# Rebuilding the first batch's key chain in a fused attention and feed-forward kernel

## The chip, the cores and the metric

The kernel runs on one core of one Trainium2 chip. The metric is the device time of one execution in microseconds (us), as a median of several executions. Before the change the median is 321.27 us over three runs (320.65 to 321.33). The profiled execution of the kernel before took 322.2 us, with a profiled span of 320.4 us. All positions below are microseconds from the start of a profiled span.

## The reference, cut to what matters

```python
# q, k, v: (4, 4, 1088, 32) float32; S1, S2: (8, 32)
def phi(x):                                   # 64 features from 32 numbers
    a = einsum('rd,bhsd->bhsr', S1, x)
    b = einsum('rd,bhsd->bhsr', S2, x)
    return einsum('bhsi,bhsj->bhsij', a, b)   # 8 x 8
kv  = sum over s of phi(k) v;  z = sum over s of phi(k)
num = phi(q) kv;  den = phi(q) z + 1e-06
x   = num / den                               # bridged to (4352, 128)
out = ((x @ w1) * (x @ w2)) @ w3 @ w_out      # d_ff = 1024
```

The sketches S1 and S2 and the weights arrive as float64 words and are converted on the chip. The denominator is the delicate part. The kernel gets z from the Gram matrix of the keys, G, the sum over s of k kᵀ, through S1 G S2ᵀ. To keep enough bits, it splits each key k into a leading part k1, rounded on a grid of eight bits, and a rest k2 = k - k1.

## The kernel before

The 1088 positions of a head are handled as 1024 "main" ones (eight chunks j of 128) and 64 "rest" ones (those of two batches share a tile). TensorE's array is used in four column groups, one for each head h. The products of a half batch (four chunks) run in this order:

```python
def products(out, lhs, rhs, start):
    for i, c in enumerate(chunks):
        for h in range(H):                       # the four column groups in turn
            nc.tensor.matmul(out[h * D:(h + 1) * D], c[lhs][rows, h], c[rhs][rows, h], ...)
products(acc["kv"], "v", "kp", first)            # float32, 64 wide
products(acc["g2"], "k2", "ks", False)           # float32, 32 wide; ks = k + k1
products(acc["g1"], "k1", "k1", False)           # bf16, 32 wide
...
nc.scalar.mul(ym, acc["g2"], 0.5)                # G = g1 + (g2 + its transpose) / 2
nc.vector.transpose(yt, ym)
```

A float32 matmul of this program leaves two records in the trace, a bf16 one leaves one. "Record" below means such a record.

Weights are converted in chunks of 128 x 512: ScalarE makes two words (cv_c, cv_m) and for most chunks a tile of signs (sgn). VectorE joins them (w, wo, w3c). The matmuls "idle_ps" multiply zeros. They exist to keep TensorE's clock up. The first two groups of queries of batch 0 are written out by hand in one fixed order (the "first part"); later groups are merged by weights.

```python
run_all([..., kv0, q_tr, kv1, kvr, lambda: idle(8), q_lead, cv[0], fin1, lambda: idle(4), sketch_P,
         cv[1], fin2, fin4, lambda: idle(4), n_nat, cv[2], cv[3], fin3, ...
         f[2], n_dens, f[3], n_phi, f[4], n_phT, f[5], n_nd])     # six of the eight pairs of group 0
run(merge([(1.7, x) for x in f[6:]] + ffn_steps(1, 16), k_steps(1), w_out))
```

## Time and profile before

| what | kernel before |
|---|---|
| median of three runs | 321.27 us |
| profiled span | 320.4 us |
| first xT (attention output of group 0) starts | 40.35 us |
| VectorE starts on the keys of batch 1 | 57.40 us |
| last transpose of a w_out chunk ends | 114.94 us |
| from there to the end | 205.46 us |
| TensorE, VectorE, ScalarE busy | 293.6, 195.3, 132.7 us |

The page divides the span into 40 slices and prints the busy share of each engine in tenths. The chain of waits is read from the end of the execution back to its start, each piece being what released the next. The table of windows gives busy microseconds of each engine in a stretch. Those lines are in the prediction below. One more table of windows matters later, which shows only the instructions that write the tile ps_kvz, that is the Gram and feature-value matmuls. These are the kernel before's lines for one half batch and for one rest (window, its length, TensorE busy with its records, weight loads, VectorE, ScalarE, clock, DMA):

```profile
145.68:146.65 0.97, 0.97 (x80) 0.84 (x64) 0.00 (x0) 0.00 (x0) 1.00 0.00 0
155.43:155.75 0.32, 0.31 (x20) 0.27 (x16) 0.00 (x0) 0.00 (x0) 1.00 0.00 0
```

Each window runs from the start of the stretch's first record to the start of the next other record. The reader should keep 0.97 us for 80 records and 0.32 us for 20: 12.1 and 16 ns a record.

### The profile page before, as it was taken

Reading aid. Unit: us, or ns where it says so; the run is one execution under the profiler, and the core shown is the slowest. Engines: PE = TensorE matmul, PEld = TensorE weight load, DVE = VectorE, ACT = ScalarE, POOL = GpSimd, SP = SyncE. Lnnn points to the kernel's source line nnn. Section 1 sums busy time; section 2 is a strip of 40 time slices with the busy share of each in tenths; the row PEclk is TensorE's granted clock in tenths of the full one; section 3 lists DMA queues with packets and bytes.
Section 4 is the critical chain, followed back from the end, with each engine's and each line's share of the span. In section 5 each row is a group of like instructions: output and inputs, shape, how many; then the busy total and the mean of one; then the engine's idle time right before and its main releaser. Section 6 shows DMA issues by size and latency. Waiting matters only on the chain.

```text
span 320.4 us, 4951 instructions
## 1 busy us (share of the span) xinstructions
PE 293.6 (92%) x1924; PEld 174.4 (54%) x1924; DVE 195.3 (61%) x495; ACT 132.7 (41%) x258; POOL 16.6 (5%) x21
## 2 busy tenths in 40 slices
PE   7866997669998999999999999999999999999992
PEld 5746553257766765465645446555454644444581
DVE  6987867996879638376846626654572572462130
ACT  4313273897998330533332253322324224323231
POOL 2200000100003000010301001000100100000000
PEclk9855699978999999999999999999999999999998
DMA  5998240375743000000000000000000000000000
GB/s 165 337 264 243 94 133 0 105 266 163 246 156 118 0 0 2 33 1 2 3 33 2 0 33 0 2 2 35 2 0 0 33 0 2 33 0 1 35 33 17
DMA packets 15064, 20.77 MB, mean 65 GB/s; under 512 B 4032, under 2 KB 11456, under 8 KB 15040
## 3 DMA queue, kind: packets, MB, share of 16 engines
q1 hardware_dynamic: 15040, 20.46, 19.9%
q8 instruction: 15, 0.25, 0.3%
q14 instruction: 9, 0.07, 0.1%
HBM read 18.22 MB, written 2.23 MB: 64 GB/s over the span
## 4 chain that ended last, share of the span: by engine, by line
PE 73%; ACT 11%; DVE 10%; issue 4%; POOL 1%; DVEq 0%; POOLq 0%
PE ps_o L740 19%; PE a_ps L727 15%; PE b_ps L731 14%; PE ps_w3o L375 3%; PE ps_x L682 3%; ACT cv_c L230 3%; PE ps_kvz L474 3%; PE ps_c L610 3%; PE ps_ph L665 2%; PE ps_c L608 2%; PE idle_ps L184 2%; ACT sgn L236 2%; PE ps_ab L424 2%; ACT cv_m L231 1%; ACT ffa L729 1%
## 5 line engine op out<-in xcount | busy, mean ns | idle before, releaser
L733 DVE TENSOR_TENSOR ab<-ffa,b_ps 128x512 f32<-128x512 f32 (+1 forms) x72 | 47.2, 655 | 62.5 <-PE b_ps L731 56.9
L729 ACT COPY ffa<-a_ps 128x512 f32<-128x512 f32 (+1 forms) x72 | 40.7, 565 | 78.3 <-PE a_ps L727 73.4
L727 PE MATMUL a_ps<-xT,w 128*128 128x512 f32 (+1 forms) x144 | 72.4, 585 | 0.7 <-ACT xT L685 0.7
L731 PE MATMUL b_ps<-xT,w 128*128 128x512 f32 (+1 forms) x144 | 70.5, 571 | 1.3 <-ACT ffa L729 1.3
L740 PE MATMUL ps_o<-ab,w3o 128*128 128x512 f32 (+1 forms) x144 | 70.3, 582 | 0.7 <-ACT ob L743 0.7
L731 PEld LDWEIGHTS b_ps<-xT,w 128*128 128x128 f32 x144 | 26.7, 190 | 29.4 <-issue 22.7
L740 PEld LDWEIGHTS ps_o<-ab,w3o 128*128 128x128 f32 x144 | 24.8, 190 | 22.6 <-issue 20.2
L727 PEld LDWEIGHTS a_ps<-xT,w 128*128 128x128 f32 x144 | 24.4, 192 | 18.0 <-issue 11.7
L375 PE MATMUL ps_w3o<-wo,w3T 128*128 128x128 f32 x128 | 18.0, 293 | 2.4 <-ACT w3T L370 1.7
L264 DVE TENSOR_REDUCE g_q<-qT 128x1 f32<-128x512 f32 (+1 forms) x9 | 5.9, 655 | 23.3 <-ACT qT L578 23.3
L375 PEld LDWEIGHTS ps_w3o<-wo,w3T 128*128 128x128 f32 x128 | 16.9, 205 | 5.5 <-ACT w3T L370 2.8
L667 ACT COPY pT<-ps_ph 128x512 f32<-128x512 f32 (+1 forms) x18 | 9.2, 565 | 15.8 <-PE ps_ph L665 15.8
L231 ACT ACTIVATE cv_m<-raw 128x512 int32<-128x512 uint32 x22 | 15.4, 698 | 0.8 <-DVE w3c L248 0.8
L230 ACT ACTIVATE cv_c<-raw 128x512 f32<-128x512 f32 x22 | 15.4, 706 | 0.0
L610 PE MATMUL ps_c<-Rl,qT 128*128 128x96 f32 (+1 forms) x72 | 15.0, 302 | 0.0
L608 PE MATMUL ps_c<-Rf,q 128*128 128x64 f32 (+1 forms) x72 | 13.2, 276 | 1.4 <-POOL q L584 1.4
L584 POOL TENSOR_TENSOR q<-qT,q 128x512 f32<-128x512 f32 (+1 forms) x6 | 6.4, 1073 | 150.1 <-DVE q L275 150.1
L608 PEld LDWEIGHTS ps_c<-Rf,q 128*128 128x128 f32 (+1 forms) x72 | 11.4, 201 | 4.3 <-issue 2.4
L236 ACT CAST sgn<-cv_c 128x512 f16<-128x512 f32 x17 | 13.4, 790 | 0.1
L184 PE MATMUL idle_ps<-zeros 128*128 128x256 bf16 x52 | 11.9, 420 | 1.6 <-DVE zeros L179 1.6
L665 PEld LDWEIGHTS ps_ph<-ident,ph 128*128 128x128 f32 x68 | 7.9, 143 | 7.6 <-issue 5.9
L432 DVE TENSOR_TENSOR kp<-ps_ab,b_sb 128x1024 f32<-128x1024 f32 x8 | 9.8, 1222 | 3.5 <-ACT b_sb L428 3.5
(169 smaller groups left out, 372.8 us busy)
## 6 DMA issues: line engine op xcount, KB each, us to landing
raw<-in_moe_w_dram SPq DMA_DIRECT2D x20, 512.0 KB, 4.5
k_sb<-in_k_dram SPq DMA_DIRECT2D x4, 512.0 KB, 5.1
v_sb<-in_v_dram SPq DMA_DIRECT2D x4, 512.0 KB, 5.8
q_sb<-in_q_dram SPq DMA_DIRECT2D x4, 512.0 KB, 6.3
out_dram<-oT SPq DMA_DIRECT2D x8, 256.0 KB, 2.0
raw<-in_moe_w_out_dram SPq DMA_DIRECT2D x2, 512.0 KB, 10.4
kr<-in_k_dram SPq DMA_DIRECT2D x4, 32.0 KB, 3.7
vr<-in_v_dram SPq DMA_DIRECT2D x4, 32.0 KB, 6.0
```

The lines of the kernel that those rows point to most:

```text
L184: nc.tensor.matmul(idle_ps[:, :n], zeros[:, :128], zeros[:, :n], start=True, stop=True)
L230: nc.scalar.mul(x["c"], hi.bitcast(F32), 2.0 ** -112)
L231: nc.scalar.mul(x["m"].bitcast(I32), lo.bitcast(U32), 2.0 ** -29)
L236: nc.scalar.copy(bview(x["s"].bitcast(F16)[:, 1:], [[2, CW]]), x["c"])
L375: nc.tensor.matmul(ps, w3T[ko][:, c], wo[:, c], start=(c == 0), stop=(c == NC - 1))
L608: nc.tensor.matmul(C[rows, :2, j], s["q2"][:, cols], cols_of(Rf, b), start=True, stop=False, skip_group_check=True)
L610: nc.tensor.matmul(C[rows, :, j], s["qT"][:, cols], cols_of(Rl, b), start=False, stop=True, skip_group_check=True)
L727: nc.tensor.matmul(a_ps[:, :n], w1[:, cols], xT[key], start=True, stop=True)
L729: nc.scalar.copy(a_sb[:, :n], a_ps[:, :n])
L731: nc.tensor.matmul(b_ps[:, :n], w2[:, cols], xT[key], start=True, stop=True)
L733: nc.vector.tensor_mul(ab[:, :n], a_sb[:, :n], b_ps[:, :n])
L740: nc.tensor.matmul(o_ps[g][:, :n], w3o[:, c], ab_sb.pop((g, c))[:, :n], start=c == 0, stop=c == NC - 1)
```

## The change

The intent is to get the first batch's state ready earlier and to take work off ScalarE. Cut to its core:

```diff
-            products(acc["g2"], "k2", "ks", False)          # f32 32 wide
-            products(acc["g1"], "k1", "k1", False)          # bf16 32 wide
+            for h in range(H):                              # for each chunk
+                products(acc["g"], h, kk[rows, 0, h], kk[rows, :, h], start=start)   # k1 x [k1|k2], f32 64 wide
+                if kf is not None:
+                    products(acc["g2"], h, kk[rows, 1, h], kf[rows, h])              # k2 x k, f32 32 wide
+                else:                                       # rest keys: k2 x k1, k2 x k2
+                    for x in range(2):
+                        products(acc["g2"], h, kk[rows, 1, h], kk[rows, x, h])
...
-            nc.scalar.mul(ym, acc["g2"], 0.5)
-            nc.vector.transpose(yt, ym)
-            nc.vector.tensor_add(ym, ym, yt)
-            nc.vector.tensor_add(gb, gb, ym)
+            nc.vector.tensor_add(gb, gb, acc["g2"])
...
-            round_to(s["q1"], s["qT"], grid(s["qT"], 128, 8, "q"))
+            nc.scalar.activation(s["q2"], s["qT"], ACT.Identity, bias=g)
+            nc.scalar.activation(s["q1"], s["q2"], ACT.Identity, bias=g, scale=-1.0)
...
-            words, join, add = convert(n, dst, n % 4 != 1)
+            words, join, add = convert(n, dst, signs=False)  # w_out chunks: no sign cast
...
-    load_raw(NRAW)                                           # then k, v, q of batch 1, rests
+    load_raw(2)                                              # the others behind a memset after G
...
+             ... f[4], n_phi, w_out[1][1], f[5], n_phT, f[6], n_nd, f[7]])   # all eight pairs
-    run(merge([(1.7, x) for x in f[6:]] + ffn_steps(1, 16), k_steps(1), w_out))
+    run(merge(ffn_steps(1, 16), k_steps(1), w_out[2:]))
```

The rest keys also share the grid of an even batch's main keys now, so their own peak and rounding go; ks goes too. The sketch's masked copies move from GpSimd to ScalarE, raw buffers go from five to six, idle matmuls from 52 to 95, and the transfer queue is pinned to the order in which the first part is written. The first part was pinned on the compute engines before too. Below, "the gate" is the memset that holds the bulk loads (weights, inputs of batch 1) back until G is done.

## The prediction

> **What bounds the kernel now.** I read the page first, for engines and slices of the span (320.4 us, so a slice is 8.0 us). Rows below: busy tenths of TensorE and VectorE, the granted TensorE clock, the DMA share.
>
> ```profile
> PE   7866997669998999999999999999999999999992
> ...
> DVE  6987867996879638376846626654572572462130
> ...
> PEclk9855699978999999999999999999999999999998
> DMA  5998240375743000000000000000000000000000
> ```
>
> TensorE is full from slice 13 on; before that it has holes, and twice half a clock. All that the change can win lies in the first 115 us. Next the chain of waits in the prologue (start, length, what), because batch 0 runs alone there.
>
> ```profile
> 14.91 1.52 PE ps_kvz L474 x77
> 16.44 2.01 issue
> 18.45 0.77 PE ps_kvz L474 x23
> ...
> 19.24 0.21 ACT ym L510
> ...
> 23.57 0.60 DVE w L242
> ...
> 25.88 0.85 PE idle_ps L184 x4
> 26.73 0.23 PE ps_N L291 x2
> ...
> 29.12 0.11 DVE Rh L542
> ...
> 29.28 0.40 PE ps_a L600 x4
> ```
>
> The last Gram matmul of batch 0 ends at 19.2 us, the state Rh at 29.2; the first attention output xT follows at 40.9. The chain holds a 2.01 us hole, a weight conversion (0.60) and idle matmuls (0.85) that do nothing for batch 0. Then the stages (window, its length, busy time of each engine, clock, DMA share):
>
> ```profile
> 57.40:67.90 10.50, 5.96 (x22) 2.75 (x20) 10.48 (x21) 10.13 (x19) 0.92 (x1) 1.00 0.50 161
> 67.90:75.30 7.40, 6.56 (x25) 5.09 (x26) 5.83 (x10) 5.68 (x11) 0.00 (x0) 0.54 0.84 274
> 75.30:103.65 28.35, 26.42 (x321) 19.26 (x320) 24.25 (x42) 26.95 (x54) 2.51 (x1) 1.00 0.52 167
> 103.65:114.94 11.29, 11.29 (x71) 8.77 (x72) 7.38 (x25) 4.22 (x9) 0.00 (x0) 1.00 0.00 0
> 114.94:320.40 205.46, 197.66 (x1112) 107.28 (x1111) 103.56 (x265) 64.75 (x128) 9.61 (x7) 0.99 0.03 12
> ```
>
> From 57.4 to 103.65 ScalarE converts weight words: 42.76 of 46.25 us busy. After 103.65 TensorE is always busy, and the last transpose of a w_out chunk ends at 114.94. What follows (205.5 us) is TensorE work, nearly unchanged. So I predict three pieces: the prologue, the middle up to that last transpose, and the rest.
>
> **What the skill says.** "TensorE: Matmul & The Clock Gate", Part 1, gives half clock after an idle window of about 3.4 us and full clock after a busy one. The trace agrees: only 1.00 and 0.50 occur in 2 us slices, with drops at 13.57 and 68.3 us, 16 windows of 3.41 apart. The 24 idle matmuls took 0.22 us each, as at half clock later (0.21), although the row shows full clock there. "Runtime: NRT & Kernel Launch", Instruction fetch mechanics, says that each engine's instructions are fetched in 16 KiB blocks over a DMA queue of its own. In the 2.01 us hole nothing is waited for, the DMA share is 1.07, and a transfer of instruction queue q8 lies in it; so I read it as a fetch stuck behind bulk loads. "TensorEngine Tiling (Array Packing)", Key Properties, says that column tiles run independently: 32 records 64 columns wide take 0.47 us start to start in the Gram part, as four groups side by side would. "GPSIMD Engine Reference", Specifications, has GpSimd share SBUF interfaces with VectorE. The trace agrees: the k2 subtraction took 3.16 us beside GpSimd's ks, 1.22 alone.
>
> **Part 1, the Gram chain of batch 0.** Removed: ks on VectorE (1.15), the rest keys' own peak and rounding, ym and its transpose and sums (0.21+0.13+0.20 and one wait, about 0.6), P's pair (1.16 from 22.41) and the weight join (0.60) between G and T, the four idle matmuls between T and N, and the 2.01 us hole if the bulk loads are gone. Added: per half of the keys, 32 float32 records 64 wide (0.47) and 32 of 32 wide (0.28) in place of 32 of 32 wide (0.28) and 16 bf16 ones (0.2), some +0.27 us at full clock. Step by step I get: k2 done at 12.1 as now, Gram sums done at about 15.9 (19.2 now), G at 17.9 (21.7), T's pair at 20.2 (25.4), Rh at 22.6 (29.2). The following attention chain (ps_a to xT, 11.6 us) ran two thirds at half clock; at full clock its matmuls lose about 1 us: xT at 33.4 instead of 40.9, so -7.5. If the clock still drops, 3 to 5 us of this come back.
>
> **Part 2, the second group.** Before, its chain runs 40.9 to 58.4 on VectorE (weight joins, split, dens, ph), with six of eight feed-forward pairs of group 0 inside, and the next stage starts at 57.4. After, all eight pairs are in, ph of group 1 should be done at about 48 (54.05), and VectorE reaches batch 1 at about 54.1. Two pairs (2 x 2 x 0.86 of TensorE) have moved ahead of that point.
>
> **Part 3, the middle.** From 57.4 to 110.5, the last w3c join, ScalarE works 45.8 us and VectorE 45.9. ScalarE loses 13 sgn casts of 0.80 (10.4) and two chunks' words of 0.71+0.70 (2.8): 32.6 stay, so it is no longer the bound. VectorE gains for each of these 13 chunks one tensor_scalar of 0.42 (+5.5) and loses ks (1.2), the collision with GpSimd (1.9), the transpose and sums (0.5), the rest keys' own steps (0.9) and two feed-forward multiplies (1.4): 45.5. TensorE's work up to 114.94 is 45.8+4.4, less 3.4 for the two moved pairs, less 3.2 for the half clock, plus 0.65 Gram and one more ps_o of 0.86: 45.1. VectorE and TensorE are thus both the bound. With no wait the stage would end at 54.1+45.5 = 99.6. With VectorE filled to the 0.86 of before (45.9 of 53.1), at 107; I choose nearer the better end, 0.91, because the cast that it waited for is gone: 54.1+50 = 104, and the last transpose at 105 instead of 114.94. Of these 9.9 us, 3.3 are the earlier start, some 1.7 the moved pairs and 5 the middle itself.
>
> **Part 4, the rest.** 205.5, less 0.86 for the ps_o already done, plus 2 x 0.65 for the Gram sums of batches 2 and 3, which lie on TensorE's path, plus up to 1 us where TensorE waits for the longer q chain (two ScalarE passes of about 0.57 in place of one VectorE pass of 0.53; two such waits of 0.7 us exist now): 206.5.
>
> **Sum.** 105+206.5 = 311.5 of profiled span against 320.4; 0.9 more for the times outside the profile (321.27 against 320.4): 312.4. Against it: raw loads and batch 1's inputs leave the first 18 us and may free more holes than the one counted. I settle on 311.5.
>
> **The rivals.** First, the clock. Idle matmuls rise from 52 to 95; at half clock, 43 more at 0.21 are 9 us of TensorE in the prologue, and those in the pauses of 13, 16 and 30 can stand before N, ps_a and split on TensorE's queue. For it: in the trace before, 24 idle matmuls did not keep the clock past 13.57. Against: pauses now lie where TensorE waits anyway, and the Gram sums are denser. It would give 315 to 318. Second, VectorE takes ScalarE's place in the middle at its old filling, or worse because joins now have two dependent passes: 107 to 109, so 313.5 to 316. Third, four records in a row on one column group (the loop over h is now outside) do not overlap with the next group: up to 2 us per half instead of 0.75, some 3 us per batch, four times, three of them in full TensorE stages: 318 to 322. Against it speaks the rest group's ps_c, where runs of four records per half of the columns overlap in this trace (280 to 281 us). Fourth, the bulk loads behind G land late: about 4.8 MB at the 350 GB/s seen between 13.6 and 18.5 need 14 us from 18, so they land before 36, and batch 1's keys are wanted at 54: hidden, no loss; the same transfers may though hit instruction fetches of 18 to 36 us, +1 to 2 us.
>
> **Range and chances.** The first piece has +5 for the clock and -1, the middle -5 (no waits) to +4, the rest 0 to +3, and these are not tied together; 8 times in 10 I expect 304.5 to 318. Faster by over 2% means below 314.8, a third of the way from my value to no change: 0.76. Within 2%: 0.21. Slower by over 2%, above 327.7, needs the third rival at full size and a cold clock together: 0.03.
>
> **What would show it.** Right: no issue piece of 2 us near 16; full clock between 13 and 37; xT of the first group near 33 to 34; ScalarE under 80% between 55 and 100 while VectorE is above 85%; last transpose of w3c near 105; from there 206 to 207 to the end. Wrong: half clock up to 37, or idle matmuls in the chain before N and ps_a (first rival); VectorE idle in the middle behind TensorE or the reverse with the transpose after 108 (second); a Gram half over 1.5 us start to start at full clock (third); ScalarE or VectorE waiting for raw (fourth). The prediction fails most likely in the middle, where I scaled sums by a filling rather than followed a chain.

## The result, and the profile after

The changed kernel is correct and takes 319.84 us (median of four runs, 319.39 to 320.62). The kernel before took 321.05 us in the same comparison. The ratio is 0.9966, with a 95% interval of 0.9942 to 0.999. Ratios here and below are the mean time of one kernel's fast runs over that of the kernel before's fast runs of the same rounds, so they are not quite the ratio of the medians. The gain is 0.3%, where the prediction had 311.5 us and a range of 304.5 to 318 us.

These are the busy tenths, the granted clock and the DMA share of the changed kernel's page (40 slices of 7.95 us, span 317.9 us):

```profile
PE   6898898589999999999999999999999999999992
...
DVE  6769785899999463686537438443661662462120
...
PEclk9999999969999999999999999999999999999998
DMA  5539893166542000000000000000000000000000
```

The long stretch of half clock at the start is gone (only one slice, near 63 to 70 us, and the last are below full), and TensorE is full from the tenth slice on instead of the fourteenth. It looks like a success of the kind that was predicted. This is the chain of waits of its prologue (start, length, what):

```profile
12.66 1.98 PE ps_kvz L508 x99
14.65 1.36 issue
16.01 1.67 PE ps_kvz L508 x61
...
17.70 0.20 DVE g_pair L276
```

The Gram sums are read at 17.70 us. A hole in which TensorE waits for nothing that the profile shows is still there, 1.36 us long. And this is the table of windows (window, its length, busy time of TensorE, its weight loads, VectorE, ScalarE and GpSimd, clock, DMA share, GB/s):

```profile
56.40:63.00 6.60, 3.25 (x16) 1.87 (x15) 6.50 (x13) 5.12 (x10) 0.00 (x0) 0.99 0.11 24
63.00:70.00 7.00, 5.49 (x75) 3.97 (x76) 7.00 (x13) 4.17 (x7) 0.00 (x0) 0.52 0.70 217
70.00:95.39 25.39, 25.39 (x304) 19.64 (x303) 24.01 (x42) 21.20 (x41) 0.00 (x0) 1.00 0.56 184
95.39:108.18 12.79, 12.79 (x83) 9.82 (x83) 10.67 (x40) 6.16 (x12) 0.00 (x0) 1.00 0.14 42
108.18:317.90 209.72, 201.97 (x1199) 109.97 (x1197) 98.44 (x248) 73.77 (x140) 6.44 (x6) 0.99 0.03 12
```

From 56 to 70 us VectorE is full and TensorE is not: from 60.32 to 64.36 us it stands still until VectorE has rounded the keys of batch 1, and its clock is half from 62.92 to 69.75 us. From 70.0 us TensorE is busy in all of 25.39 and 12.79 us: from here on nearly every microsecond of TensorE work is a microsecond of time. The last transpose of a w_out chunk ends at 108.18 us, 6.8 us earlier than before. The rest then takes 209.72 us, 4.3 us longer than the 205.46 of before. The difference, 2.5 us, is the difference of the two spans. The medians differ by less, because the profiled execution of the kernel before was a slow one of its kind (322.2 us).

Step by step:

| step | before | predicted | changed kernel | behind the prediction |
|---|---|---|---|---|
| Gram sums read | 19.2 | 15.9 | 17.7 | 1.8 |
| first xT ends | 40.94 | 33.4 | 35.11 | 1.7 |
| features of group 1 (ph) done on VectorE | 54.05 | 48 | 50.81 | 2.8 |
| VectorE starts on batch 1's keys | 57.40 | 54.1 | 57.43 | 3.3 |
| last transpose of w_out ends | 114.94 | 105 | 108.18 | 3.2 |
| from there to the end | 205.46 | 206.5 | 209.72 | 3.2 |
| time outside the span | 1.8 | 0 | 1.8 | 1.8 |

Two stretches deserve to be looked at. The first lies between the first xT and batch 1: of 5.8 us gained at the first xT, 3.2 are left when VectorE has done ph of group 1, and none when it reaches batch 1's keys. This is VectorE's timeline in the changed kernel (start, length, line, instruction, idle time before it and what ended it):

```profile
49.52 1.29 DVE L726 TENSOR_TENSOR ph<-ay,bs 128x512 f32<-128x512 f32 x2
...
53.57 0.69 DVE L803 TENSOR_TENSOR ab<-ffa,b_ps 128x512 f32<-128x512 f32 x1 [2.16 <-PE b_ps L801]
56.49 0.69 DVE L803 TENSOR_TENSOR ab<-ffa,b_ps 128x512 f32<-128x512 f32 x1 [2.23 <-PE b_ps L801]
...
57.43 1.21 DVE L276 TENSOR_REDUCE g_k<-k_sb 128x1 f32<-128x1024 f32 x1
```

And this is the same step in the kernel before:

```profile
56.80 0.69 DVE L733 TENSOR_TENSOR ab<-ffa,b_ps 128x512 f32<-128x512 f32 x1 [2.16 <-PE b_ps L731]
57.40 1.21 DVE L264 TENSOR_REDUCE g_k<-k_sb 128x1 f32<-128x1024 f32 x1
```

In the changed kernel VectorE stands still for 2.16 and 2.23 us, waiting for the last two products of group 0, although it could work on the keys of batch 1; the kernel before has one such wait there. The second is the length of the last stage. These are the ps_kvz matmuls in it, first of the kernel before, then of the changed one:

```profile
114.94:320.40 205.46, 4.95 (x360) 3.88 (x288) 1.76 (x8) 0.40 (x2) 0.99 0.03 12
```

```profile
108.18:317.90 209.72, 9.02 (x448) 7.39 (x448) 2.14 (x10) 0.99 0.03 12
```

For batches 2 and 3 the Gram and feature-value matmuls take 9.02 us of TensorE instead of 4.95. That is 4.1 of the 4.3 us by which the stage grew; the prediction allowed 1.3. One half's Gram, one half's feature-value product and one rest of the changed kernel:

```profile
145.30:146.23 0.93, 0.93 (x64) 0.88 (x64) 0.00 (x0) 1.00 0.00 0
147.28:147.87 0.59, 0.59 (x32) 0.49 (x32) 0.00 (x0) 1.00 0.00 0
149.78:150.67 0.89, 0.89 (x32) 0.80 (x32) 0.00 (x0) 1.00 0.00 0
```

A half costs 1.52 us instead of 0.97 and a rest 0.89 instead of 0.32.

### The profile page after: what moved, and what is told of

Read it like the earlier page. It is cut to its first block, busy times and chain, and to the rows that moved or that the text cites. A ratio compares the mean times of both kernels' runs of the same rounds, so it can differ in the third digit from the quotient of the medians.

```text
span 317.9 us, 5394 instructions
## 1 busy us (share of the span) xinstructions
PE 296.4 (93%) x2143; PEld 176.8 (56%) x2143; DVE 188.0 (59%) x482; ACT 141.6 (45%) x277; POOL 7.1 (2%) x12
## 3 DMA queue, kind: packets, MB, share of 16 engines
HBM read 18.22 MB, written 2.23 MB: 64 GB/s over the span
## 4 chain that ended last, share of the span: by engine, by line
PE 82%; DVE 9%; ACT 4%; issue 2%; POOL 1%; POOLq 0%; DVEq 0%; ACTq 0%
PE ps_o L810 19%; PE a_ps L797 18%; PE b_ps L801 15%; PE ps_kvz L508 5%; PE ps_w3o L403 5%; PE ps_wt L396 3%; PE ps_x L752 3%; PE ps_c L675 2%; PE ps_ab L452 2%; PE ps_c L673 2%; PE ps_ph L735 2%; PE idle_ps L190 2%; PE ps_ot L820 1%; ACT q L644 1%; ACT q L645 1%
## 5 line engine op out<-in xcount | busy, mean ns | idle before, releaser
L403 PEld LDWEIGHTS ps_w3o<-wo,w3T 128*128 128x128 f32 x128 | 15.7, 192 | 3.4 <-issue 2.6
L737 ACT COPY pT<-ps_ph 128x512 f32<-128x512 f32 (+1 forms) x18 | 9.2, 565 | 18.5 <-PE ps_ph L735 18.5
L403 PE MATMUL ps_w3o<-wo,w3T 128*128 128x128 f32 x128 | 16.0, 275 | 0.0
L673 PE MATMUL ps_c<-Rf,q 128*128 128x64 f32 (+1 forms) x72 | 12.4, 263 | 2.6 <-POOL q L649 1.5
L190 PE MATMUL idle_ps<-zeros 128*128 128x256 bf16 x95 | 13.1, 295 | 1.7 <-DVE zeros L185 1.7
L675 PE MATMUL ps_c<-Rl,qT 128*128 128x96 f32 (+1 forms) x72 | 13.9, 284 | 0.0
L673 PEld LDWEIGHTS ps_c<-Rf,q 128*128 128x128 f32 (+1 forms) x72 | 10.4, 185 | 5.5 <-POOL q L649 2.4
L508 PE MATMUL ps_kvz<-kk 128*32 128x64 f32 x256 | 8.6, 236 | 4.0 <-DVE kk L492 4.0
L190 PEld LDWEIGHTS <-zeros 128*128 128x128 bf16 x95 | 10.0, 108 | 3.4 <-DVE zeros L185 1.7
```

Of the source, the lines that this page charges most:

```text
L190: nc.tensor.matmul(idle_ps[:, :n], zeros[:, :128], zeros[:, :n], start=True, stop=True)
L403: nc.tensor.matmul(ps, w3T[ko][:, c], wo[:, c], start=(c == 0), stop=(c == NC - 1))
L508: nc.tensor.matmul(out[h * D:(h + 1) * D], lhs, rhs, start=start, stop=stop, skip_group_check=True)
L673: nc.tensor.matmul(C[rows, :2, j], s["q2"][:, cols], cols_of(Rf, b), start=True, stop=False, skip_group_check=True)
L675: nc.tensor.matmul(C[rows, :, j], s["qT"][:, cols], cols_of(Rl, b), start=False, stop=True, skip_group_check=True)
```

## The experiments

My theory after the result had two parts. First, the new Gram form (k1 x [k1|k2] and k2 x k in float32) costs TensorE what the chain gains, either by the order of its records (four to six in a row on one column group) or by the form itself (more float32 work, more separate stretches). Secondly, something between the first xT and batch 1 absorbs the prologue's gain. The rivals were the bulk transfers' gate, the detour of q over ScalarE (two passes there for one on VectorE), the idle matmuls, and the moved sign casts. All twelve runs gave correct results. Each was timed in five rounds. Starts that are compared between runs carry some noise: the first Gram record starts at 12.3 to 13.4 us in the changed kernel and its variants.

### The order of the Gram records: e1_h_inside and e2_before_h_outside

In e1 the changed kernel goes through the heads before the next product.

```diff
-            for h in range(H):
-                products(acc["g"], h, ...)
-                products(acc["g2"], h, ...)       # for each chunk
+            for i, (kk, kf) in enumerate(chunks):
+                for h in range(H):
+                    products(acc["g"], h, ...)
+            for kk, kf in chunks:
+                for h in range(H):
+                    products(acc["g2"], h, ...)
```

> The changed kernel with one edit: its Gram products go through the four heads (the four column groups) before the next product or chunk, as the kernel before did, instead of staying four records (six in the rest) on one head. In the changed kernel a half's Gram stretch takes 0.93 us for 64 records, its rest stretch 0.89 us for 32 records (before: 0.97 for 80 records with kv, 0.32 for 20). Theory A (order costs: records of one column group in a row do not overlap): the Gram stretch of a half falls to about 0.75, the rest to about 0.45, 0.8 us per batch; three of the four batches lie where TensorE never waits, so some 2.5 us of the changed kernel's 319.8 go: ratio to the kernel before about 0.988. Rival B (the amount of float32 work costs, whatever its order): stretches and time unchanged, ratio 0.996.

Measured: 318.92 us against 320.84 of before in the same rounds, ratio 0.9933 (0.9908 to 0.9959). These are one half's Gram, its feature-value product and one rest:

```profile
144.65:145.53 0.88, 0.88 (x64) 0.84 (x64) 0.00 (x0) 1.00 0.00 0
146.59:147.17 0.58, 0.58 (x32) 0.49 (x32) 0.00 (x0) 1.00 0.00 0
149.09:149.57 0.48, 0.48 (x32) 0.39 (x32) 0.00 (x0) 1.00 0.00 0
```

The rest falls from 0.89 to 0.48 us as expected: with its Gram records six in a row on one head a record costs 27.8 ns on the mean, and 15.1 with the heads inside. The half falls only from 0.93 to 0.88, not to 0.75. The last stage fell from 209.72 to 208.66 us, what its ps_kvz matmuls lost (9.02 to 7.97). Order is a true cost, but the smaller one. Why it costs the rest so much more than the half is open: in the rest the edit also parts two products that add into the same columns, which was not run apart.

In e2 the kernel before gets the bad order.

```diff
-            products(acc["g2"], "k2", "ks", False)
-            products(acc["g1"], "k1", "k1", False)
+            for i, c in enumerate(chunks):
+                for h in range(H):
+                    for out, lhs, rhs in ((acc["g2"], "k2", "ks"), (acc["g1"], "k1", "k1")):
+                        nc.tensor.matmul(out[h * D:(h + 1) * D], ...)
```

> The kernel before with one edit: its Gram products k2 x ks and k1 x k1 stay on one head for a chunk (three records in a row on one column group) instead of going through the four heads. Theory A (order): a half's stretch of 80 records grows from 0.97 us by 0.15 to 0.3, the rest's from 0.32 by 0.2, and the time by 1 to 2 us (ratio 1.003 to 1.006). Rival B (order is free): 1.000 and the same stretches.

Measured: 321.45 us, ratio 1.0018 (0.9994 to 1.0043). Its half stretches take 1.02 instead of 0.97 us, and its rests 0.32 as before. The effect of three records in a row is 0.05 us per half, under what was expected, and the time cannot be told from no change.

### The gate of the bulk transfers: e4_bulk_ungated and e9_before_gated

In e4 the changed kernel starts all loads at once.

```diff
-            if i == 2:
-                nc.vector.memset(raw[i].bitcast(I32)[:1, :1], 0)
+    load_more()                                   # directly behind load_raw(2)
...
-             sketch_R, sketch_Pa, fin1, load_more, next_in,
+             sketch_R, sketch_Pa, fin1, next_in,
```

> The changed kernel with its bulk transfers started at once instead of behind the Gram matrix of batch 0 (queue order stays). If holes of instruction fetch come from bulk transfers, the issue piece of 1.36 us at 14.65 grows to 2 us or more, k and v of batch 0 do not change, xT of the first group comes 0.5 to 2 us later than 34.5 and the time grows by 0 to 2 us (ratio 0.997 to 1.003). If the gate delays the weights more than it helps, the joins after 31 us come earlier and the time falls by up to 1 us.

Measured: 326.95 us, ratio 1.0175 (1.0147 to 1.0204), far outside what I expected. This is its chain of waits at the hole:

```profile
13.01 1.98 PE ps_kvz L506 x94
15.00 4.12 issue
19.11 0.92 PE ps_kvz L506 x34
```

The hole is 4.12 us. After it the clock is at 0.57 on average from 18 to 34 us (1.00 in the changed kernel), and the first xT comes at 42.1 us instead of 34.5. The transfers of the instruction queue q8 go with the length. (q8 moves 15 packets of 16 KiB in the kernel before and 17 in the changed one, in step with TensorE's records, 3848 and 4286.) In the changed kernel one starts at 13.78 us and takes 0.96 us, and no other packet starts in the hole; in e4 the same transfer starts at 16.57 us, beside bulk loads at 368 GB/s, and takes 1.02 us. So it was the start that came late. In the kernel before, the changed one and e4, TensorE goes on 1.3 to 1.5 us after this transfer has landed; why so late is not shown. The gate is worth about 7 us to the changed kernel.

In e9 the kernel before gets the gate and the pinned queue, and nothing else.

```diff
-    load_raw(NRAW)
-    load_in("k", 1)
-    ...
+    load_raw(2)
+    def load_more(): ...                          # called in fin1 of batch 0, behind a memset
```

> The kernel before with one part of the change alone: only two raw loads at the start, the other bulk loads after the Gram matrix of batch 0, transfer queue in given order. Ungating the changed kernel cost 7 us (hole of 4.12 us, clock at half from 18 to 34). If the gate is what gains, the hole of 2.01 us at 16.44 shrinks to 1.4 or less and the first xT comes 1 to 5 us before 40.4: 316 to 320 us, ratio 0.985 to 0.997. Rival: the kernel before has its weight joins (from 23.6 us) so early that late raw loads stop VectorE: ratio 1.00 or above.

Measured: 320.53 us, ratio 0.9973 (0.9954 to 0.9992). The hole goes: the q8 transfer had landed at 14.70 us, and TensorE, held up by VectorE, passes record 222 only at 16.4. But the Gram sums are still read at 18.5 us because VectorE is late there, and the first xT comes at 39.4 instead of 40.35. The gate alone is worth little without the shorter chain; the shorter chain is worth nothing without the gate.

### The idle matmuls: e6_no_pauses

```diff
-    pause = lambda n: lambda: idle(n)
+    pause = lambda n: lambda: None
```

> The changed kernel without the idle matmuls of its pauses (71 of 95; the 24 at the start stay). If the pauses hold the clock, half clock comes back between 14 and 37 us, xT of the first group comes 2 to 5 us later than 34.5 and the time grows by as much (ratio 1.003 to 1.012). If they only stand in TensorE's queue (the first rival of the prediction), xT comes earlier and the time falls by up to 1.5 us (0.992). Also: in nine traces TensorE stops for nothing after matmul record 221 (222 in the kernel before). If it runs out of fetched instructions, a count decides: with 7 idle matmuls fewer ahead of the Gram stretch the hole stays after record 221, that is 7 records later within the stretch.

Measured: 321.47 us, ratio 1.0013 (0.9988 to 1.0039). The clock is at 0.55 from 18 to 34 us and the first xT comes at 37.2 us. The pauses thus earn 1.6 us, and the first rival of the prediction was wrong about the changed kernel. This is its chain at the hole:

```profile
12.39 2.09 PE ps_kvz L508 x108
14.48 1.34 issue
```

The hole stays behind matmul record 221, now 160 records into the Gram stretch instead of 153: later by the seven idle matmuls that it no longer runs before. Counted with the weight loads and the semaphore instructions in the trace, TensorE has run 449 records when it stops, in all eleven traces in which the profile names no cause for the stop (e9 has none; in e10 and e12 TensorE waits for VectorE there). A wait for data would not keep such a count. With the transfers of q8 it says that TensorE runs out of fetched instructions: it had come to record 221 before the next block was there, and in e9, where it came later than the block, it did not stop.

### The rounding of q: e5_q_round_dve

```diff
-            nc.scalar.activation(s["q2"], s["qT"], ACT.Identity, bias=g)
-            nc.scalar.activation(s["q1"], s["q2"], ACT.Identity, bias=g, scale=-1.0)
+            round_to(s["q1"], s["qT"], g)
```

> The changed kernel with the rounding of q back on VectorE (one tensor_scalar of 0.53 us in place of two ScalarE passes of 0.73 in the chain). If the ScalarE detour lengthens the chain of groups 0 and 1, xT of group 0 comes 0.9 us earlier than 34.5 and the DVE chain of group 1 too; each wait of TensorE for GpSimd's q2 (0.8 and 0.7 us) goes: in all 1 to 2 us less (ratio 0.991 to 0.994). Rival: VectorE, full from 56 to 70 us, pays for it and nothing changes (0.996).

Measured: 319.03 us, ratio 0.9947 (0.991 to 0.9984). That overlaps with the changed kernel's 0.9966. The trace is sharper than the time. From the first xT to the second it takes 19.31 us, 20.03 in the changed kernel, so the detour costs 0.7 us in the second group. In the first group taking it out brought nothing: the first xT came at 35.6 us.

### The sign casts: e3_signs_kept

```diff
-            words, join, add = convert(n, dst, signs=False)
+            words, join, add = convert(n, dst, n % 4 != 1)
```

> The changed kernel with the sign casts of the w_out chunks kept on ScalarE as before (12 casts of 0.80 us back on ScalarE, 12 tensor_scalar of 0.42 us off VectorE). My prediction had VectorE as the bound of the middle: if so, the time falls by 1 to 3 us (ratio 0.987 to 0.993). If ScalarE would be the bound again, it rises by 1 to 3 us (1.00 to 1.006). If TensorE alone bounds the stage after 70 us, nothing changes (0.996) but the stretch of 56 to 70.

Measured: 320.76 us, ratio 0.9982 (0.9965 to 0.9999), not clearly different from the changed kernel. ScalarE becomes full again from 80 to 95 us (14.75 of 15.00 us) and TensorE gets small holes there (14.69 of 15.00). So relieving VectorE of a pass per chunk brought nothing behind 70 us, where TensorE is full in the changed kernel. What dropping the casts was worth is not settled: 0.5 us by the ratios, 0.9 by the medians, and the intervals overlap.

### The old Gram form for batches 2 and 3: e7_old_gram_late and e8_old_gram_q_dve

In e7 the order is that of e1, and batches 2 and 3 use the kernel before's form. For lack of room e7 and all runs built on it (e8, e10 to e12) have five raw buffers, not six.

```diff
+        old = b >= 2
...
+                if old:
+                    nc.vector.tensor_sub(k1, x, k1s[n])           # k2, from k1 in bf16
+                    nc.gpsimd.tensor_add(k2, x, k1s[n])           # ks
...
+        if b >= 2:
+            st.append((1.3, lambda: kvs(0, feats[0][1])))         # kv, k2 x ks, k1 x k1 in one stretch
```

> The changed kernel with the heads inside (as e1_h_inside) and, for batches 2 and 3 alone, the Gram form of the kernel before (k2 x ks in float32, k1 x k1 in bf16, ks on GpSimd, one stretch of kv and Gram per half); five raw buffers instead of six for lack of room. Theory A (the new form's TensorE work takes the gain back): Gram and kv of those batches fall from 4.2 us to the 2.26 of the kernel before each, so 3.8 us less than the changed kernel, plus 0.5 from batch 1: 315.5 us, ratio 0.983. Rival (TensorE's Gram time is not what was lost; GpSimd's ks collides with VectorE or the waits move elsewhere): no better than e1_h_inside, 0.993.

Measured: 316.38 us, ratio 0.9863 (0.9832 to 0.9894). These are the ps_kvz matmuls of its last stage:

```profile
109.89:315.20 205.31, 4.95 (x360) 3.88 (x288) 1.76 (x8) 0.40 (x2) 1.00 0.03 12
```

The 4.95 us of the kernel before are back, and with them a last stage of 205.31 us. The time fell by somewhat less than the stage, since in the profiled run the last transpose came later (109.9 us against 108.2, and 107.6 in e1); whether the missing raw buffer did that was not run apart. The theory that the Gram form takes the gain back holds for this part.

e8 adds the rounding of q on VectorE, as in e5.

> e7_old_gram_late and the rounding of q on VectorE as in e5_q_round_dve. e5 alone was 0.2% below the changed kernel, within noise; if that is real and adds up, ratio 0.981; if VectorE pays elsewhere, the same as e7 (0.983).

Measured: 315.51 us, ratio 0.9827 (0.9802 to 0.9853). The step from the first xT to the second is again 19.3 us instead of 20.0. The time is lower than that of e7 by 0.9 us, with overlapping intervals.

### The Gram before the features: e10_kv_after_gram and e11_T_before_kv

e10 is e8 with the Gram sums ahead of the feature-value products in batch 0.

```diff
-             gs0, kp0, gs1, kp1, q_nat, kv0, r_kp, kv1, kvr, q_tr, pause(5),
-             sketch_R, sketch_Pa, fin1, load_more, ...
+             gs0, gs1, kgr, kp0, kp1, r_kp, q_nat, fin1, kv0, kv1, kvr, q_tr, pause(5),
+             sketch_R, sketch_Pa, fin1b, load_more, ...
```

> e8_old_gram_q_dve with one more edit in batch 0: the Gram products of main and rest keys come first, VectorE starts on G, and the products of features and values (72 records) run beside that. The Gram sums need 152 records instead of 224 before G, with the hole still after record 221, so g_pair starts at about 16.7 instead of 17.7 us and the first xT at 34 instead of 34.9: 1 us less than e8 (ratio 0.980) if the gain of the prologue is handed on through the chain of the second group and batch 1's keys; 0.983 if it is lost there.

Measured: 314.92 us, ratio 0.9799 (0.978 to 0.9818). The time cannot be told from e8's. The Gram sums were read at 15.5 us, but the first xT came at 35.06: in TensorE's order T stood behind the feature-value products, which waited until VectorE had read G (they start at 17.13 us), and behind q's transposes, so T began at 19.74 us.

e11 puts T directly behind G.

```diff
-             ... r_kp, q_nat, fin1, kv0, kv1, kvr, q_tr, pause(5), ..., T_mm, sketch_Pb, kz, pause(13), T_pair, N_mm, ...
+             ... r_kp, q_nat, q_tr, sketch_R, sketch_Pa, sketch_Pb, fin1,
+             T_mm, kv0, kv1, kvr, pause(5), T_pair, fin1b, load_more, next_in, N_mm, kz, q_grid, q_lead, pause(20), ...
```

> e10_kv_after_gram handed almost nothing on (first xT 21.6 us after the first Gram record, 21.8 in e8): its chain shows why, the 72 records of features and values, the transposes of q and the hole still stood ahead of T in TensorE's order, so T started at 19.74 although G was ready at 17.1. Here T comes directly behind G (q's transposes and P's pair before G, features and values behind T, N ahead of kz). If that order was what lost it, T starts at about 17.5, the first xT comes 1.5 to 2 us earlier (about 20 after the first Gram record) and the time falls by about as much: ratio 0.974 to 0.977. If the prologue's gain is absorbed later, by VectorE's full stage before 70 us, the time stays at 0.980. The hole stays after TensorE record 449 (matmul record 220 or 221) in any case.

Measured: 316.18 us, ratio 0.9822 (0.9798 to 0.9846). This was a miss. T began at 18.0 us, and then the chain shows this:

```profile
22.68 4.27 PE idle_ps L190 x20
...
27.12 0.44 DVE g_ay L740
```

The clock fell (0.67 on average from 18 to 24 us), the 20 idle matmuls took 0.21 us each instead of 0.11, and they stood ahead of ps_a, which the chain needs next, in TensorE's queue. Here the prediction's first rival came true after all.

### The keys of batch 1 in VectorE's gap: e12_keys1_in_gap

e12 is e10 with one move: the first three steps of batch 1's keys come between the last products of group 0.

```diff
-             w_out[0][1], n_dens2, f[4], n_phi, w_out[1][1], f[5], n_phT, f[6], n_nd, f[7]])
+             w_out[0][1], n_dens2, f[4], n_phi, w_out[1][1], f[5], k1_peak, n_phT, f[6], k1_first, k1_second, n_nd, f[7]])
```

> e10_kv_after_gram with peak, rounding and remainder of batch 1's keys placed on VectorE between the last feed-forward products of group 0, where VectorE in the changed kernel waits 2.16 and 2.23 us for TensorE (50 to 56.5 us). In the changed kernel VectorE starts on these keys at 57.43 us, in the kernel before at 57.40: the 5.8 us that the first xT had gained are gone there, because the fixed order put all eight products of group 0 ahead. If that order is what lost them, the keys start at about 51.5, the Gram matmuls of batch 1 start 3 us earlier than 64.2, TensorE runs without a stop from about 67 to 68 instead of 70, and the time falls by 1.5 to 3 us: ratio 0.971 to 0.975. Rival: the stage after it is bound by VectorE's whole sum or by ScalarE's words, so only the order of work changes: 0.980.

Measured: 312.14 us against 320.98 in the same rounds, ratio 0.9711 (0.9683 to 0.9738), inside what was expected. This is VectorE's timeline:

```profile
50.79 1.21 DVE L276 TENSOR_REDUCE g_k<-k_sb 128x1 f32<-128x1024 f32 x1
53.03 0.69 DVE L859 TENSOR_TENSOR ab<-ffa,b_ps 128x512 f32<-128x512 f32 x1 [1.03 <-PE b_ps L857]
...
54.86 1.23 DVE L505 TENSOR_TENSOR kk<-k_sb,kk 128x1024 f32<-128x1024 f32 x1
56.00 0.68 DVE L859 TENSOR_TENSOR ab<-ffa,b_ps 128x512 f32<-128x512 f32 x1
```

The keys of batch 1 start at 50.8 instead of 57.4 us and fill the second wait and half of the first. The first Gram matmul of batch 1 starts at 58.9 us (64.2 in e10), and the last transpose of w_out ends at 106.2 us. This is the fastest version, 2.9% under the kernel before.

## Why the prediction was wrong

**The bound.** Right: what the change could win lay in the first 115 us, and what follows was TensorE work. Half clock between 13 and 37 us went, as written. The second and fourth rivals did not decide anything. The measured time lies inside the 318 to 322 us of the third rival, but by luck: it asked for a Gram half over 1.5 us, and a half took 0.93. One reading was loose: not all slices of 2 us in the kernel before show 1.00 or 0.50; those with a switch in them lie between (0.55 to 0.89), and only the trace's list of clock changes has just the two.

**Part 1, the prologue.** The step "the 2.01 us hole if the bulk loads are gone" failed. I had read the hole as a fetch stuck behind bulk loads. The runs show a stop after a fixed count of records, 1.36 us long even when no other transfer runs, and 4.12 us with the bulk loads (e4, e6): the loads lengthen it and do not make it. It is 1.36 of the 1.8 us by which the Gram sums came late. The first xT ended 1.7 us behind, so the chain after the Gram sums held (17.4 us for a predicted 17.5), and the size of this part was -5.8 instead of -7.5 us.

**Part 2, the second group.** The step that failed is "ph of group 1 should be done at about 48": it was done at 50.81. Of these 2.8 us, 1.7 came with the first xT. Of the other 1.1, the detour of q over ScalarE, which I had charged only to the last part, is 0.7 (e5, and e8 against e7). From there to batch 1's keys I had allowed 6.1 us, 2.75 more than before, for the two moved pairs, and it took 6.6; with that VectorE was there at 57.43 and not at 54.1. So VectorE's waits of 2.16 and 2.23 us are not what I missed in size. What I had not seen is that this time need not be lost: the order alone put the keys behind the waits, and moving them into the waits gave 2.8 us from e10 to e12, each by its median.

**Part 3, the middle.** From the start on batch 1's keys to the last join it took 46.3 us for a sum that I had put at 45.5, and VectorE was busy 44.4 of these: fuller than the 0.91 that I chose. But the last transpose ended 4.4 us behind the last join where I had put one: in the kernel before it is 110.58 to 114.94 us, 4.4 too. TensorE, full in both, has other work in its order between the two, 16 records of a w_out product (1.95 us) and a pair of feed-forward products among them. The stage took 50.7 us where I had 50.9, with its two terms wrong in opposite ways: that the stage fitted is luck. ScalarE was no longer the bound, as predicted (34.5 of 46.3 us busy); from 70.0 us on TensorE was, busy in all of the stretch, and taking a pass per chunk off VectorE gained nothing there (e3).

**Part 4, the rest.** The term "2 x 0.65 for the Gram sums of batches 2 and 3" was mis-sized: it measured 9.02 - 4.95 = 4.1 us. The third rival named the effect, and I gave it too small a chance, and only one of its causes. Of the 4.1 us, e1 takes away 1.05 by the order of the heads; e7 takes away the other 3.0 by the old form. There are more records (448 against 360), and they stand in twelve stretches instead of six. In the kernel before and in the changed one the 32 feature-value records of a half start over the same 0.435 us; but inside the joint stretch the next record follows 0.04 us later, and 0.15 us later where they are a stretch of their own. So they take 0.47 and 0.59 us. In e1 the 64 Gram records start over 0.75 us, the figure that I had, and the next record follows 0.13 us later. I took costs read inside a joint stretch for matmuls that no longer run in one. A half of e1 takes 0.49 us more than the kernel before's (0.88 and 0.58 against 0.97): 0.11 is the feature-value product's own end, 0.38 the Gram form with its end. The first half of batch 2 even falls into three Gram stretches. Form and splitting were not run apart.

**The sum.** The span came out 6.4 us above the predicted 311.5: 3.2 before the last transpose and 3.2 after it. Another 1.8 us is the time outside the span (319.66 against 317.9 us in the profiled execution). I had added 0.9 for it, from a median and a span of different executions, and then dropped it in settling on a round value.

## What to carry to other kernels

When a chain is shortened early in a program, follow the gain to the first place where a fixed instruction order makes an engine wait for something else: here 2.6 of 5.8 us went in a longer chain of the second group and the other 3.2 in front of the next batch's keys, and moving the three steps of these keys into VectorE's waits brought back 2.8. A form that shortens latency for the first batch should not be given to later batches that run where TensorE never waits; there only its busy time counts. And count records, not only microseconds: here small matmuls outran the fetch of instructions, and bulk loads under way at that moment made the stop three times as long (4.12 us against 1.36).

## What the Trainium skill lacked or had wrong

- "Runtime: NRT & Kernel Launch", Instruction fetch mechanics, calls the crossing of a block boundary mostly hidden and gives as reason that instructions are issued more slowly than the blocks arrive. Here TensorE stopped after 449 of its records in eleven traces: for 1.1 to 1.6 us in the changed kernel and its variants with the gate, 1.6 and 2.01 us in two forms of the kernel before, and 4.12 us in e4, where the block's transfer started late beside bulk loads at 368 GB/s. The page doesn't say what bulk loads do to a fetch, nor that TensorE goes on only 1.3 to 1.5 us after the block has landed.
- "TensorEngine Tiling (Array Packing)", Key Properties, says that tiles run independently, but gives no price for records that follow each other on one tile. A rest with its Gram records six in a row on one column group took 27.8 ns a record, 15.1 with the four groups in turn. For a half, four in a row, it was 14.5 against 13.7 ns.
- The same section says that changing the tiling mode drains TensorE, without a price. After the last of 32 feature-value records the next record started 0.04 us later inside a stretch of column tiles and 0.15 us later where a matmul on the whole array came next. That agrees with a drain of about 0.1 us, which was not measured by itself.
- "TensorE: Matmul & The Clock Gate", Part 1, agrees with every trace on its two states (only 1.00 and 0.50). It doesn't say what idle matmuls cost when the clock falls all the same: 20 of them took 4.27 us in the chain of e11, while in the changed kernel 71 of them saved 1.6 us.
